# Eighty-two products of zeros between the warm-up and the first real product of a fused attention and gated feed-forward kernel

## The chip, the core and the metric

The kernel runs on one core of a Trainium2 chip. Its time is the device time of one execution in microseconds (us). The engines are TensorE (PE in the profile, its weight loads PEld), VectorE (DVE), ScalarE (ACT), GpSimd (POOL) and SyncE (SP, here a queue for DMAs alone); each runs its own instructions in order, and they wait for each other by semaphores.

## The reference

`x` has 2048 tokens of 448 numbers. Attention with 16 heads of 28 and a gated feed-forward block of width 1792 both read the same `x`; a gate per token mixes the two. All data are float32.

```python
x = A_x
g = _sigmoid((x * gate_w).sum(-1, keepdims=True))
# attention: 16 heads of 28
qkv = x @ wqkv
scores = einsum("bhqd,bhkd->bhqk", q, k) * 28 ** -0.5
o = einsum("bhqk,bhkd->bhqd", softmax(scores), v)
a = o @ wo
# feed-forward, 448 -> 1792 -> 448
gate = x @ W_gate
gate = gate * (gate > 0)
b = (gate * (x @ W_up)) @ W_down
return g * a + (1 - g) * b
```

## The kernel before

**Two forms of product.** A float32 product can go to TensorE in two ways here. In the split form a number is written as a high and a low part, each in a rounded 32-bit type (`F32R` in the code), and a product is the sum of three such products: high by high, low by high, high by low. Contractions over 448 rows take 11 instructions (`TERMS`, with the last half chunk packed). In the exact form the operands are plain float32 (`F32`, or `f32(...)`, which reads a rounded tile as float32), and one call of `matmul` does the whole product. The kernel uses the exact form only for probabilities by values (line 692, tile `po`): there the stationary operand is 32 columns wide, and four heads' blocks, j = 0 to 3, go to four strips of 32 partitions of one PSUM bank. `pv` runs for 32 visits (16 heads, two halves of the keys each) in two parts of 4 chunks by 4 blocks: 32 x 2 x 16 = 1024 calls of `matmul`.

**Stages.** (1) A warm-up: 11 bf16 products of a zeroed tile `warm` (line 496), which nobody reads. (2) Projections: `qk(tb, c)` makes 128 rows of queries and keys for a block of 512 tokens in 11 split products (line 454), `vproj` the values (line 469). What they read, `W` and `X`, is loaded by DMA and split into high and low parts by ScalarE (`act_high`, line 136) and VectorE (`low`, line 142); `split_first` does this chunk by chunk for the first block. (3) 32 rounds, one per head and half of the keys, whose order on TensorE is written out by hand in the strings `R0` to `R31`: score products (line 330), products for the row maxima (line 224), products of the feed-forward layer (line 633), and the exact ones (line 692). (4) The rest of the feed-forward layer (`down_mm`, line 927) and the output projection (line 886).

**What sets the order at the start.** Nothing is reordered: each engine gets its instructions in the order of the calls. Behind the warm-up come, on POOL, the identity matrix, four memsets of `K[0]`, `QS[0]`, `K[1]`, `QS[1]` (lines 503 and 504), eight memsets of `V` (lines 506 and 507), and behind those the DMAs that send the first projections to DRAM (lines 464 and 363). `QS[1]` holds the queries of head 1 later on. On ScalarE and VectorE come `split_first`, `split_w(*w1)`, then the two copies of the first projection out of PSUM (high part and low part, to `K[2]`, which serves as a staging buffer), and behind these the splits of the next blocks of `x`. The banks of PSUM: a pool `mx` of two tiles of two banks (used from the first row maxima on), `x` and `s` of two banks each. `ps_x("warm_ps")` takes a bank of `x`.

Of the kernel before, what the change touches and what calls it, by code (L numbers as in the profile page):

```python
# [8 lines left out]
F32 = mybir.dt.float32  # L9
# [9 lines left out]
P = 128  # L19
# [9 lines left out]
TB = 512  # L29
# [70 lines left out]
def gated_mix_kernel(ctx, tc, x, wq, wo, wgu, wd, out):  # L100
    nc = tc.nc
# [3 lines left out]
    psum = ctx.enter_context(tc.tile_pool(name="psum", bufs=1, space=PSUM))  # L105
# [3 lines left out]
    def f32(ap):  # L109
        return ap.bitcast(F32)  # L110
# [53 lines left out]
    QS = [vp.tile([P, 4, TB], F32R, name=f"Q{r}") for r in range(2)]  # L164
# [200 lines left out]
    with tc.tile_pool(name="qkv", bufs=1) as pa:  # L365
# [128 lines left out]
        ps = ps_x("warm_ps")  # L494
        for n in range(WARM):
            nc.tensor.matmul(ps, warm[:, :P], warm, start=True, stop=True)

        ident = const.tile([P, P], F32, name="ident")
        make_identity(nc, ident)
# [37 lines left out]
        for n, (f, *a) in enumerate(mixed):  # L537
# [29 lines left out]
            among, was = [], m  # L567
# [207 lines left out]
    for v, order in enumerate(ROUNDS):  # L775
# [4 lines left out]
        for o in order:  # L780
# [12 lines left out]
            elif o == "x":  # L793
                i, half, n = passes.pop(0)
# [228 lines left out]
```

## Time and profile before

| | |
|---|---|
| median of 2 runs | 1184.8 us (1184.59 to 1185.01) |
| profiled execution, device time | 1184.21 us |
| its span, first to last instruction | 1182.4 us |
| TensorE busy | 1175.0 us, 99% of the span |
| VectorE, ScalarE, GpSimd busy | 894.1, 877.2, 743.3 us |
| granted TensorE clock, mean | 0.999 |
| mean HBM traffic | 159 GB/s over the span |

How to read it: a line of a timeline gives the start and the length in us, the engine, the line of the kernel, the operation, output and input tiles, shapes, how many instructions were merged (x...), and in brackets how long the engine had been idle before and what ended that. Instructions of TensorE are pipelined: a product's own length (some 400 ns for a split one) is longer than the distance from its start to the next one's start, so costs are taken from such distances, or from a run of many products divided by their count.

### The profile page before, as it was taken

What the parts mean: (1) busy time and instruction counts of PE and PEld (TensorE: products, weight loads), DVE (VectorE), ACT (ScalarE), POOL (GpSimd) and SP (SyncE); (2) the same over time, 40 slices, a digit from 0 to 9 for tenths busy, and PEclk for the clock granted to TensorE, in tenths of its full rate; (3) what the DMA queues carried; (4) which work ended last, traced back from release to release, by engine and by line L of the source; (5) the groups of instructions that cost most, each with busy time, mean ns of one, the idle gap of its engine ahead of it and who ended that gap; (6) DMA issues with size and microseconds to landing.
All of it is one profiled execution on the core that took longest, in us unless ns stands there. A gap on an engine that the chain in (4) does not pass through costs nothing.

```text
span 1182.4 us, 17006 instructions
## 1 busy us (share of the span) xinstructions
PE 1175.0 (99%) x6183; PEld 821.2 (69%) x6183; DVE 894.1 (76%) x1173; ACT 877.2 (74%) x1054; POOL 743.3 (63%) x325
## 2 busy tenths in 40 slices
PE   9999999999999999999999999999999999999998
PEld 6886666666666666666666666666666667899997
DVE  6577898888988898989898888889898553444242
ACT  5237889899999988888888887888888885322121
POOL 5323667888988886777777766767676784422020
PEclk9999999999999999999999999999999999999999
DMA  9994565636373754343446535153444437644342
GB/s 322 280 394 142 186 210 172 185 124 196 117 216 108 205 167 139 119 128 92 119 136 212 140 102 153 49 152 109 139 154 156 129 100 231 209 152 118 115 134 75
DMA packets 70667, 188.85 MB, mean 160 GB/s; under 512 B 13958, under 2 KB 20558, under 8 KB 65678
## 3 DMA queue, kind: packets, MB, share of 16 engines
q1 hardware_dynamic: 65624, 167.31, 45.9%
q0 software_dynamic: 4480, 19.99, 4.5%
q8 instruction: 48, 0.79, 0.3%
q10 hardware_dynamic: 480, 0.47, 0.1%
q14 instruction: 35, 0.29, 0.1%
HBM read 126.96 MB, written 60.96 MB: 159 GB/s over the span
## 4 chain that ended last, share of the span: by engine, by line
PE 96%; DVE 1%; DMA 1%; ACT 1%; issue 0%; SPq 0%; DVEq 0%; ACTq 0%
PE gu L633 24%; PE s L330 20%; PE po L692 19%; PE acc L927 12%; PE sm L224 10%; PE v L469 3%; PE wo L886 3%; PE qk L641 3%; PE qk L454 2%; DVE r L280 1%; DMA wr<-wq 0%; DMA X<-x_d 0%; ACT P L336 0%; ACT V L336 0%; SPq L414 0%
## 5 line engine op out<-in xcount | busy, mean ns | idle before, releaser
L309 POOL TENSOR_TENSOR P<-P,rm 128x2048 f32<-128x2048 f32 x102 | 470.8, 4635 | 107.9 <-DVE rm L303 84.1
L633 PE MATMUL gu<-X,wg 128*128 128x512 f32 x1232 | 358.9, 395 | 0.1
L228 DVE TENSOR_REDUCE mx<-sm 128x1 f32<-128x1024 f32 x256 | 302.9, 1217 | 43.0 <-PE sm L224 42.1
L330 PE MATMUL s<-Q,K 128*128 128x512 f32 x1024 | 315.9, 403 | 1.7 <-DVE mx L228 0.9
L633 PEld LDWEIGHTS gu<-X,wg 128*128 128x128 f32 x1232 | 231.2, 188 | 57.6 <-issue 1.7
L330 PEld LDWEIGHTS s<-Q,K 128*128 128x128 f32 x1024 | 180.7, 188 | 82.4 <-DVE r L280 10.4
L336 ACT ACTIVATE P<-s 128x1024 f32<-128x1024 f32 x204 | 202.2, 1028 | 42.0 <-PE s L330 39.6
L692 PE MATMUL po<-P,V 128*32 128x512 f32 x1640 | 227.4, 594 | 0.0
L334 ACT ACTIVATE P<-s 128x1024 f32<-128x1024 f32 x206 | 201.4, 1040 | 14.1 <-PE s L330 13.1
L320 ACT ACTIVATE P<-P 128x1024 f32<-128x1024 f32 (+1 forms) x182 | 208.5, 1171 | 0.5 <-POOL P L309 0.2
L224 PE MATMUL sm<-K,Q 128*128 128x512 f32 x520 | 163.2, 400 | 0.1
L280 DVE SCALAR_TENSOR_TENSOR r<-s,r 128x1024 f32<-128x1024 f32 x124 | 151.6, 1223 | 13.6 <-ACT P L336 6.0
L692 PEld LDWEIGHTS po<-P,V 128*32 128x32 f32 x1640 | 62.6, 110 | 113.3 <-issue 109.6
L692 PE MATMUL po<-V 128*32 128x512 f32 x408 | 136.2, 594 | 0.0
L309 POOL TENSOR_TENSOR V<-V,rm 128x2048 f32<-128x2048 f32 x24 | 111.2, 4635 | 26.1 <-DVE rm L303 22.6
L224 PEld LDWEIGHTS sm<-K,Q 128*128 128x128 f32 x520 | 91.9, 188 | 34.1 <-ACT P L334 4.6
L136 ACT ACTIVATE hh<-hr 128x512 fp32r<-128x512 f32 x52 | 32.8, 632 | 109.5 <-PE acc L927 109.4
L142 DVE TENSOR_TENSOR hh<-hr,hh 128x512 fp32r<-128x512 f32 x52 | 47.3, 915 | 72.6 <-ACT hh L136 72.5
L927 PE MATMUL acc<-WD,hh 128*128 128x448 f32 x480 | 99.5, 366 | 0.0
L927 PEld LDWEIGHTS acc<-WD,hh 128*128 128x128 f32 x480 | 90.2, 188 | 7.3 <-DVE hh L142 0.2
L280 DVE SCALAR_TENSOR_TENSOR r<-s,P 128x1024 f32<-128x1024 f32 x50 | 61.1, 1223 | 33.3 <-ACT P L336 33.0
L295 DVE TRANSPOSE_TENSOR_REDUCE mn<-r 128x32 f32<-128x1024 f32 x63 | 78.1, 1239 | 1.3
(93 smaller groups left out, 1135.5 us busy)
## 6 DMA issues: line engine op xcount, KB each, us to landing
wg<-ws_d SPq DMA_DIRECT2D x42, 896.0 KB
K<-qk_d SPq DMA_DIRECT2D x32, 448.0 KB
X<-x_d SPq DMA_DIRECT2D x56, 256.0 KB
h_d<-h SPq DMA_DIRECT2D x56, 256.0 KB
Q<-qk_d SPq DMA_DIRECT2D x62, 224.0 KB
hr<-h_d SPq DMA_DIRECT2D x52, 256.0 KB
ws_d<-wg SPq DMA_DIRECT2D x14, 896.0 KB
x_d<-X POOLq DMA_DIRECT2D x8, 1024.0 KB, 15.2
```

Of the source, the lines that this page charges most:

```text
L224: nc.tensor.matmul(ps[:, c, :], Q[h][:, u * P:(u + 1) * P], K[h % 3][:, k0:k0 + TB], start=True, stop=True)
L228: nc.vector.tensor_reduce(to, ps, axis=AX.XY, op=OP.max)
L280: nc.vector.scalar_tensor_tensor(r, ps, -1.0, before, op0=OP.mult, op1=OP.min)
L295: nc.vector.tensor_reduce(MN[:, 1:3], R2.pop((v, j)).rearrange("p a (b r) -> p a b r", r=32), axis=AX.X, op=OP.min, apply_transpose=True)
L309: nc.gpsimd.tensor_tensor(QUAD[q], QUAD[q], m, op=OP.subtract)
L320: nc.scalar.activation(q, q, AF.Exp, scale=-SCALE)
L330: nc.tensor.matmul(ps[:, c], K[h % 3][:, k * P:(k + 1) * P], Q[h][:, j * TB:(j + 1) * TB], start=True, stop=True)
L334: nc.scalar.activation(dst, ps, AF.Exp, scale=SCALE)
L336: nc.scalar.activation(dst, ps, AF.Copy, scale=-1.0)
L633: nc.tensor.matmul(ps, WS[i][:, s, a], xf(i // NF, b), start=(n == 0), stop=(n == NT - 1))
L692: nc.tensor.matmul(po[32 * j:32 * j + 32], V[:, h // 4 % 2, k, h % 4], AT.pop((v, k, j)), start=(k == k0), stop=(k == k0 + NK // 2 - 1))
L927: nc.tensor.matmul(ACC[i // NF][t][:, :D], HH[i][:, a, t * P:(t + 1) * P], wd_high_low(f, b), start=(f == 0 and n == 0), stop=(f == NF - 1 ...
```

## The change

Behind the 11 warm-up products TensorE gets 82 calls of `matmul` more, in nine lots, ahead of the first real product. All read `z`, a quarter of `QS[1]` (128 x 512), which VectorE sets to zero first; they write the two tiles of the pool `mx`, and nobody reads what they write. In order: 8 split ones with 128 stationary columns; 8 exact ones of 128 columns; 4 split; 8 times four exact ones of 32 columns, in four strips of columns; 4 split; 8 times two exact ones of 64 columns, in two strips; 4 split; 4 exact ones of 32 columns, all in the first strip; 2 split. Each has 512 moving columns. That is 22 split and 60 exact ones (8 + 32 + 16 + 4).

```diff
         ps = ps_x("warm_ps")
         for n in range(WARM):
             nc.tensor.matmul(ps, warm[:, :P], warm, start=True, stop=True)
+
+        z = QS[1][:, 0]
+        nc.vector.memset(f32(z), 0.0)
+        four = [psum.tile([P, 2, TB], F32, tag="mx", bufs=2, name=f"four_{k}") for k in range(2)]
+        four = [t[:, k] for t in four for k in range(2)]
+
+        def tiles(z, columns, count, among=1):
+            for n in range(count):
+                for k in range(among):
+                    c = slice(k * columns, (k + 1) * columns)
+                    nc.tensor.matmul(four[n % 4][c], z[:, c], z, start=True, stop=True)
+
+        for t, columns, count, among in ((z, P, 8, 1), (f32(z), P, 8, 1), (z, P, 4, 1), (f32(z), 32, 8, 4), (z, P, 4, 1),
+                                         (f32(z), 64, 8, 2), (z, P, 4, 1), (f32(z), 32, 4, 1), (z, P, 2, 1)):
+            tiles(t, columns, count, among)
 
         ident = const.tile([P, P], F32, name="ident")
         make_identity(nc, ident)
```

On TensorE, at the program's start, the last warm-up product is followed before by the first projection (`qk_0`, which reads `X` and `W`):

```order
L496 LDWEIGHTS warm
L496 MATMUL warm_ps<-warm 128x512
L454 MATMUL qk_0_199<-X_119,W 128x512 x2
L454 MATMUL qk_0_199<-X_120,W 128x512
L454 MATMUL qk_0_199<-X_119,W 128x512 x2
```

and now by the products of zeros (`Q_108` is `QS[1]`; rows of split and exact ones of 128 columns read alike, and the first number of a shape is the count of stationary columns). From the middle of the fourth lot on, without the last two split ones, they are:

```order
L507 MATMUL four_157<-Q_108 32x512 x8
L507 MATMUL four_158<-Q_108 32x512 x8
L507 MATMUL four_157<-Q_108 128x512 x2
L507 MATMUL four_158<-Q_108 128x512 x2
L507 MATMUL four_157<-Q_108 64x512 x4
L507 MATMUL four_158<-Q_108 64x512 x4
L507 MATMUL four_157<-Q_108 64x512 x4
L507 MATMUL four_158<-Q_108 64x512 x4
L507 MATMUL four_157<-Q_108 128x512 x2
L507 MATMUL four_158<-Q_108 128x512 x2
L507 MATMUL four_157<-Q_108 32x512 x2
L507 MATMUL four_158<-Q_108 32x512 x2
```

What moved: all of TensorE's real work stands behind these rows, in its old order.

On POOL, at the same place, with the semaphores that a row waits for in brackets, before:

```order
L503 MEMSET K_105 32x2048
L504 MEMSET Q_108 32x2048
L506 MEMSET V 128x64x4 [waits Pool_49]
L507 MEMSET V 128x64 [waits Pool_49]
L506 MEMSET V 128x64x4
```

and now:

```order
L518 MEMSET K_105 32x2048
L519 MEMSET Q_108 32x2048 [waits DVE_49,PE_49]
L521 MEMSET V 128x64x4 [waits Pool_49]
L522 MEMSET V 128x64 [waits Pool_49]
L521 MEMSET V 128x64x4
```

The order on POOL is the old one, but the memset of `QS[1]` now waits for TensorE, because it overwrites a part of `z`; the memsets of `V` and the first DMAs to DRAM stand behind it in the same queue.

## The prediction

> **What bounds the kernel now.** I read the page first: busy shares, slices, and the chain that ended last.
>
> ```profile
> span 1182.4 us, 17006 instructions
> PE 1175.0 (99%) x6183; PEld 821.2 (69%) x6183; DVE 894.1 (76%) x1173; ACT 877.2 (74%) x1054; POOL 743.3 (63%) x325
> ...
> PEclk9999999999999999999999999999999999999999
> ...
> PE 96%; DVE 1%; DMA 1%; ACT 1%; issue 0%; SPq 0%; DVEq 0%; ACTq 0%
> ```
>
> TensorE is busy for 99% of the span and 96% of the chain: the kernel is as long as TensorE's queue. Whatever is put into that queue lengthens the kernel by its own time, unless TensorE would have waited then. So two things have to be found: what the 82 products take, and which waits of TensorE they cover. For the waits, first the timeline of the start, then the waits of TensorE from 10.4 us to the end:
>
> ```profile
> 0.87 0.27 DVE L493 MEMSET warm<- 128x256 uint32 x1 [0.87 <-PEq L1016]
> 1.20 4.88 PE L496 MATMUL warm_ps<-warm 128*128 128x512 bf16 x11 [1.20 <-DVE warm L493]
> 5.51 3.72 PE L454 MATMUL qk<-X,W 128*128 128x512 f32 x10
> 9.39 0.83 PE L454 MATMUL qk<-X,W 128*128 128x512 f32 x2 [0.16 <-DVE X L142]
> 10.41 27.98 PE L454 MATMUL qk<-X,W 128*128 128x512 f32 x120 [0.20 <-DVE W L142]
> ...
> PE s L330 <- DVE mx L228: 0.9, 1, 0.9
> PE s L330 <- DVE mn L590: 0.4, 1, 0.4
> PE s L330 <- ACT P L334: 0.2, 1, 0.2
> ```
>
> The first 12 real products are strung out from 5.51 to 10.41 us, because ScalarE and VectorE still split their operands. The 13th starts at 10.41; from there 120 run without a hole, and TensorE waits for only some 1.5 us in all the rest. The 13th product is therefore the mark: what it starts later, everything behind it starts later.
>
> **What one added product costs.** *Split, 128 columns.* The same form fills the row at 10.41: 27.98 / 120 = 0.233 us from one to the next. Early on it is slower. The same tile's rows in two windows of 1.2 us (the columns are PE, PEld, DVE and ACT busy time with counts, then clock and DMA):
>
> ```profile
> 5.50:6.70 1.20, 1.19 (x2) 0.95 (x3) 0.00 (x0) 0.00 (x0) 1.00 1.03 366
> 6.70:7.90 1.20, 1.20 (x7) 0.89 (x5) 0.00 (x0) 0.00 (x0) 1.00 1.03 347
> ```
>
> Two products, then seven: the profile has no clock sample ahead of that, but the warm-up's 11 in 4.88 us are about 0.43 us apart, and up to about 6.7 us everything goes at roughly half speed. The warm-up's tile is zeros too, so zeros wake the clock.
>
> *Exact.* No row shows an exact product of 128 or 64 columns in this kernel; the nearest are those of 32 columns in four strips (line 692):
>
> ```profile
> L692 PE MATMUL po<-P,V 128*32 128x512 f32 x1640 | 227.4, 594 | 0.0
> L692 PE MATMUL po<-V 128*32 128x512 f32 x408 | 136.2, 594 | 0.0
> ...
> 143.10 7.00 PE po L692 x64
> ...
> 113.63 0.40 PE L641 MATMUL qk<-X,wb 128*128 128x512 f32 x1
> 113.96 3.64 PE L692 MATMUL po<-P,V 128*32 128x512 f32 x32
> 117.42 0.61 PE L692 MATMUL po<-V 128*32 128x512 f32 x3
> 117.44 0.59 PE L692 MATMUL po<-P,V 128*32 128x512 f32 x1
> 117.85 0.60 PE L692 MATMUL po<-V 128*32 128x512 f32 x3
> 117.87 0.59 PE L692 MATMUL po<-P,V 128*32 128x512 f32 x1
> ...
> 120.44 0.59 PE L692 MATMUL po<-V 128*32 128x512 f32 x1
> 120.44 0.59 PE L692 MATMUL po<-P,V 128*32 128x512 f32 x1
> 120.97 0.27 PE L236 MATMUL mt<-ident,m 128*8 128x128 f32 x1
> ```
>
> 1640 + 408 = 2048 rows, but the code calls line 692 only 1024 times: an exact product is two records. And the records come in steps of four, one per strip: 117.42, 117.85, one step each 0.43 us (64 records, 16 steps, in 7.00 us). So the four strips run side by side, and a strip's product takes two steps, 0.86 us. Changing the form costs a little: the step at 113.96 starts 0.33 us behind a split product, not 0.233; and 120.97 is 0.53 behind the last step, not 0.43. That is 0.10 us for each change.
>
> For four strips of 32 columns this is a row of the very form that is added. Four strips together are the whole width of 128, so I take two steps of 0.43 us for one of 128 columns as well. The bound below is two records at the split form's spacing, 0.47; the bound above adds a weight load in front of each record, 0.188 us by the rows that follow, 1.24. For two strips of 64 I take two steps for the pair, between 0.47 and, one behind the other, 1.72. The four single ones of 32 columns share a strip, so each must follow the one before: 0.86 each. The Trainium skill ("FP8 and Floating Point Precision", TensorE Precision Notes) says that true FP32 takes four passes through the array, whatever the width; four half-steps of 0.215 us make the same 0.86, though no row of before shows it at 64 or 128 columns.
>
> Weight loads: are they hidden?
>
> ```profile
> L330 PEld LDWEIGHTS s<-Q,K 128*128 128x128 f32 x1024 | 180.7, 188 | 82.4 <-DVE r L280 10.4
> L692 PEld LDWEIGHTS po<-P,V 128*32 128x32 f32 x1640 | 62.6, 110 | 113.3 <-issue 109.6
> ...
> 114.42 0.13 PEld L692 LDWEIGHTS po<-P,V 128*32 128x32 f32 x4 [0.30 <-issue]
> 114.84 0.13 PEld L692 LDWEIGHTS po<-P,V 128*32 128x32 f32 x4 [0.30 <-issue]
> ```
>
> Four loads lie at the head of each step, under the products that have just begun (a step is 0.43 us either way), and a load of 0.188 us plus a product would not fit into the split form's 0.233. So yes. The Trainium skill ("TensorE: Matmul & The Clock Gate", Part 3, The mechanism) speaks against that: a weight load overlaps a running product only where their row groups differ, and all of these use all 128 rows. By that rule every load would show, and the real split products could not be 0.233 us apart; the trace disagrees, and I let the rule stand only for the exact ones of 64 and 128 columns, which no row shows (a rival below).
>
> **The sum.** The last warm-up product starts at about 1.20 + 10 x 0.427 = 5.47, so the first added one can start at about 5.9 (VectorE zeroes `z` right after `warm`, whose memset took 0.27 us; it is there long before). From 5.9:
>
> - 22 split: two before 6.7 at 0.43, 20 at 0.233: 0.86 + 4.66 = 5.5 us.
> - 8 exact of 128: 16 steps. 8 fours of 32: 16 steps. 8 pairs of 64: 16 steps. 4 single ones: 8 steps. 56 x 0.43 = 24.1 us.
> - 8 changes of form at 0.10: 0.8 us.
>
> Together 30.4 us; the first real product starts at about 36.3. All its operands have been split for 25 us by then (the wait at 10.41 was the last), so 12 products take 12 x 0.233 = 2.8 us and the 13th starts at 39.1 instead of 10.41: 28.7 us later. The cover is 1.7 us (from 5.9 to 10.41 there were 4.5 us for 2.8 us of work); nothing else of the 30.4 us is hidden.
>
> **What else moves.** The memset of `QS[1]` on POOL waits for the last product of zeros, and behind it queue the memsets of `V` and the first DMAs to DRAM:
>
> ```profile
> 6.60 1.81 POOL L504 MEMSET Q<- 32x2048 f32 x1
> 8.47 0.32 POOL L506 MEMSET V<- 128x256 f32 x1
> ...
> 10.31 0.21 POOL L507 MEMSET V<- 128x64 f32 x1
> 12.15 0.82 POOL L464 DMA_DIRECT2D qk_d<-K  x1 [1.62 <-DVE K L142]
> ...
> 10.20 0.58 ACT L136 ACTIVATE K<-qk 128x512 fp32r<-128x512 f32 x1
> 11.14 0.69 DVE L142 TENSOR_TENSOR K<-qk,K 128x512 fp32r<-128x512 f32 x1
> ```
>
> From 6.60 to 10.52 that is 3.9 us, so POOL is free 4 us after the first real product's start. What its DMA then waits for comes after 11 x 0.233 = 2.6 us of products, 0.1 until ScalarE sees them, and 1.6 from 10.20 to VectorE's end at 11.83: 4.3 us. The DMA is not late, and if it were by a few tenths, nobody reads its data before the row maxima, which stand behind all projections of queries and keys. ScalarE and VectorE stand still behind the first projection's copies, which now come 28 us later, so the splits of the next blocks gain no lead; distances from there on are the old ones. Of the 1.5 us of later waits, which end on VectorE's and ScalarE's answers to TensorE, I count nothing as saved; at best 1.5.
>
> **Total.** Span 1182.4 + 28.7 = 1211.1; the profiled execution lies 1184.21 - 1182.4 = 1.8 us above its span: 1212.9. The median of the runs is 0.6 above that execution's time, so a run should read about 1213, +2.4%. A difference of 2%, 23.7 us (1208.5), is about what a measurement of this kernel can surely tell from no change. My own case runs from 1210 (later waits saved, no cost for a change of form, half a microsecond of clock) to 1216 (the clock wakes up to 3 us later, at half a microsecond each; 0.02 us more for each wide record).
>
> **Rivals.**
>
> - *Not slower by 2%: wide exact records stream like split ones.* The 0.43 us step may belong to four separate strips that share something, not to the record. If a record of 128 or 64 columns takes 0.233, the 16 + 16 steps lose 32 x 0.197 = 6.3 us: 1206.6. It decides once the wide steps save 4.5 us together. For it: no row shows such a record. Against: the record `mt` (a transpose, 8 columns, 128 moving) lasts 0.27 us and a `po` one, with 512 moving, 0.59: 0.32 us for 384 columns more is the same 0.43 per 512, without any other strip beside it. Chance 0.09.
> - *Two strips of 64 don't run side by side.* Then 16 steps more, 6.9 us: 1219.9. Against: four strips do. Chance 0.08.
> - *Weight loads of wide exact records show.* 16 x 0.188 for 128 columns, 16 x about 0.149 (between the two rows) for 64: 5.4 us, 1218.4. Chance 0.05.
> - *The clock falls during the four single products*, which occupy a quarter of the columns for 3.4 us. As at the start it would take some 5.5 us (1.20 to 6.7) to come back, at half speed: 2.7 us, and up to 1.7 for the singles themselves: up to 1217. No row of before has TensorE so thinly used for so long. Chance 0.05.
> - *The products are dropped, as nobody reads them.* The order has all rows; 0.01, at 1185.
>
> **Numbers.** My case has 0.72, at 1213. The range must leave out no more than 0.2: from 1206, which takes in the cheap wide records, to 1219, which takes in the visible loads and the clock and ends short of the pairs in series. Faster by 2%: 0.01 for what I haven't thought of. Same: the first rival, the last, and its neighbourhood: 0.11. Slower: 0.88.
>
> **What would show it.** In the profile after: 142 more TensorE records (22 + 2 x 60), starts 0.43 us apart in the exact lots of 128 and 64, four strips' records at one time in the fourth lot, the first real product at about 36 us, no wait ahead of the 13th, POOL's first DMA within half a microsecond of VectorE's copy, and the same distances as before from there to the end. A start of the first real product before 32 us, or a wait of TensorE of over 1 us between 40 and 75 us, would make the prediction wrong.

## The result, and the profile after

The changed kernel takes 1215.9 us (1215.88 to 1215.93, two runs) against 1184.8 (1184.59 to 1185.01): a ratio of 1.026, 95% interval 1.024 to 1.028. The forecast was 1213, between 1206 and 1219.

The page of the changed kernel, the rows that answer to those of before:

```profile
span 1214.1 us, 17294 instructions
PE 1204.1 (99%) x6325; PEld 831.9 (69%) x6325; DVE 895.7 (74%) x1174; ACT 877.4 (72%) x1054; POOL 743.8 (61%) x325
...
PE 92%; DMA 3%; DVE 2%; ACT 1%; issue 1%; SPq 0%; POOL 0%; ACTq 0%; DVEq 0%; POOLq 0%
```

TensorE has 142 records more (6325 - 6183), as many weight loads, and 29.1 us more of busy time. But its share of the chain that ended last fell from 96% to 92%, and DMAs rose to 3%. A share of the chain is not a length of waiting, but it hints that not all of the 31.7 us that the span grew by are products. The timeline of TensorE at the start, and POOL's rows behind its new wait:

```profile
1.20 4.02 PE L496 MATMUL warm_ps<-warm 128*128 128x512 bf16 x11 [1.20 <-DVE warm L493]
4.87 30.46 PE L507 MATMUL four<-Q 128*128 128x512 f32 x142
35.16 11.03 PE L454 MATMUL qk<-X,W 128*128 128x512 f32 x47
...
35.38 1.81 POOL L519 MEMSET Q<- 32x2048 f32 x1 [28.71 <-PE four L507]
...
39.55 0.83 POOL L464 DMA_DIRECT2D qk_d<-K  x1 [0.23 <-issue]
```

The zeros fill 4.87 to 35.16 us, 30.3 us. The same by lots, as busy time of TensorE in nine windows (the count includes a record that reaches in from the window before):

```profile
4.86:6.89 2.03, 2.02 (x8) 1.00 1.07 359
6.89:13.99 7.10, 7.10 (x18) 1.00 0.74 262
13.99:14.77 0.78, 0.78 (x4) 1.00 0.00 0
14.77:21.78 7.01, 7.01 (x66) 1.00 0.01 2
21.78:22.90 1.12, 1.12 (x8) 1.00 0.00 0
22.90:29.92 7.02, 7.02 (x33) 1.00 0.00 0
29.92:31.04 1.12, 1.12 (x6) 1.00 0.00 0
31.04:34.59 3.55, 3.55 (x9) 1.00 0.00 0
34.59:35.16 0.57, 0.57 (x3) 1.00 0.00 0
```

In order: 8 split; 8 exact of 128 columns (16 records, and the first split one behind them); the rest of 4 split; 8 fours of 32; 4 split; 8 pairs of 64; 4 split; 4 single ones; 2 split. The exact lots of 128, of four strips and of two strips cost the same, 7.0 us each, 0.43 us a step. The split lots between strips take 1.12 us, though four split products take 0.92 elsewhere (0.231 each).

The waits of TensorE, the view that shows what the sum did not have:

```profile
PE acc L942 <- DVE hh L142: 1.6, 1, 1.6
PE warm_ps L496 <- DVE warm L493: 1.2, 1, 1.2
PE s L330 <- DVE mx L228: 0.9, 1, 0.9
PE gu L648 <- DMA X<-x_d: 0.8, 1, 0.8
PE sm L224 <- DMA Q<-qk_d: 0.7, 1, 0.7
```

Three of these (`acc`, `gu`, `sm`) are new (the prediction shows the waits of before); the one on `warm` and the one on `mx` are before's. If each real product's start is set against that of before, the 13th comes 27.5 us later, and the distance then jumps at three places: by 0.65 at 74 us, where the first row maxima wait for a load of queries (46 us by the clock of the profile before); by 0.95 at 449 us (420), where the feed-forward products wait for the next block of `x`; and by 2.1 at 1161 to 1164 us (1131), where the down projection waits for hidden values; 0.4 is won back between. From there to the end it grows by 0.9 more without any wait. The last run of products on the chain, before and after, in the chain of work in order of time (start, us, what, how many):

```profile
1144.52 34.06 PE acc L927 x168
```

```profile
1175.56 34.73 PE acc L942 x168
```

The same 168 products take 0.67 us longer, 0.207 instead of 0.203 us each. It ends at 31.7.

### The profile page after: what moved, and what is told of

It reads as the page before. It is cut to its first block, busy times and chain, and to the rows that moved or that the text cites. A ratio compares the mean times of both kernels' runs of the same rounds, so it can differ in the third digit from the quotient of the medians.

```text
span 1214.1 us, 17294 instructions
## 1 busy us (share of the span) xinstructions
PE 1204.1 (99%) x6325; PEld 831.9 (69%) x6325; DVE 895.7 (74%) x1174; ACT 877.4 (72%) x1054; POOL 743.8 (61%) x325
## 4 chain that ended last, share of the span: by engine, by line
PE 92%; DMA 3%; DVE 2%; ACT 1%; issue 1%; SPq 0%; POOL 0%; ACTq 0%; DVEq 0%; POOLq 0%
PE gu L648 23%; PE s L330 19%; PE po L707 19%; PE sm L224 10%; PE acc L942 10%; PE wo L901 3%; PE qk L656 3%; PE four L507 2%; PE v L469 2%; DVE r L280 1%; DMA Q<-qk_d 1%; DMA hr<-h_d 1%; ACT P L336 0%; DMA ox<-x 0%; DMA X<-x_d 0%
## 5 line engine op out<-in xcount | busy, mean ns | idle before, releaser
L228 DVE TENSOR_REDUCE mx<-sm 128x1 f32<-128x1024 f32 x256 | 302.6, 1216 | 44.3 <-PE sm L224 43.5
```

The costliest lines, as they stand in the source:

```text
L228: nc.vector.tensor_reduce(to, ps, axis=AX.XY, op=OP.max)
```

## Experiments: where the last 4 us come from

That the products cost 30.3 us can be read off the trace. Open was why three waits far behind them are new. Theory A, called D in the later runs: the delay shifts later DMAs in a fixed way. B: POOL's new wait. C: chance. The runs of one set share their runs of the kernel before.

**The changed kernel once more, and the kernel before once more.** No edit.

> The changed kernel once more. TensorE's first 13 real products come 27.5 us later than before in the first profile, the span is 31.7 us longer; the other 4.2 us are three waits that before has not (at about 74, 449 and 1161 us). Theory A (the delay shifts later DMAs in a fixed way): the same three waits within 0.2 us each, 1216. Theory B (the memset of QS[1] on POOL, which waits for the zeros, makes the first DMAs late): the same, 1216. Theory C (chance: DMAs land earlier or later from one execution to the next): other waits at other places, the time between 1212 and 1218.

> The kernel before once more. A and B: 1184.8, no wait of TensorE over 0.3 us at 46, 420 and 1131 us. C: some wait of half a microsecond or more at a place where the first profile has none. In all cases the clock, which woke at 6.7 us before and 4.2 us after, may wake at another time; 1 us of it is 0.5 us of the time.

Measured: 1215.7 us, ratio 1.026 (1.025 to 1.028), and 1185.3, ratio 1.000 (0.999 to 1.001). The repeated changed kernel waits at the same three places, for 1.0, 1.7 and 1.0 us; the repeated one of before has nothing there. The places are fixed, the sizes are not: C falls as an account of the places, and A's "within 0.2 us" fails.

**Zeros from another tile.**

```diff
-        z = QS[1][:, 0]
+        z = K[2][:, :TB]
```

> The zeros lie in K[2], which is next written behind the first projection in any case, so that POOL's memsets wait for nothing; TensorE's products are the same. A: 1216, the three waits stay. B: the waits go, 1212. C: 1212 to 1218, waits at other places than in the repeated run.

Measured: 1215.0 us (1213.8 to 1217.2), ratio 1.026 (1.024 to 1.028). POOL's memset no longer waits, and the waits at the loads of queries (0.9 us) and of `x` (1.3) are there; the third was absent in this execution. B falls: POOL's new wait costs nothing that can be measured, as forecast.

**The same delay in split form alone.**

```diff
-        for t, columns, count, among in ((z, P, 8, 1), (f32(z), P, 8, 1), (z, P, 4, 1), (f32(z), 32, 8, 4), (z, P, 4, 1),
-                                         (f32(z), 64, 8, 2), (z, P, 4, 1), (f32(z), 32, 4, 1), (z, P, 2, 1)):
+        for t, columns, count, among in ((z, P, 131, 1),):
```

(and `z` in `K[2]` as above).

> 131 split products of zeros (from K[2]) in place of the 82 calls: 131 x 0.2315 = 30.3 us, the same delay in one form. A: 1216 with the same three waits. B: 1212. C: 1212 to 1218. If the exact form leaves something behind that costs later, it is under 1213 and r2 is not.

Measured: 1213.2 us (1212.5 to 1213.3), ratio 1.024 (1.022 to 1.025): 2.5 us less than the changed kernel, with only 0.4 us less of zeros (29.9 us). The third wait was gone, the one for `x` 0.6. Neither form nor delay was an obvious reason, so I looked at what else differed, and found the instructions themselves.

**A new theory, F: the fetches of instructions.** The DMA queues of the page, before and after:

```profile
q8 instruction: 48, 0.79, 0.3%
...
q8 instruction: 50, 0.82, 0.3%
```

0.79 MB in 48 packets is 16 KB a packet; TensorE's records of before, 6183 products and as many loads, make 12366 instructions, 258 for each packet. So a packet brings TensorE some 256 instructions, and comes after every 128 products or so. The pages of the runs below bear this out: the queue has 48 packets with nothing added, 49 with 28 or 256 instructions more, and 50 with 262 to 290. The changed kernel has 2 x 142 = 284 more, one packet and 28 instructions (called the remainder below), so all later packets come some 14 products earlier in the work. In the changed kernel one of them falls on the moment at which a load of 1 MB of values (`V<-v_d`) ends, which by the clock of the profile before is 414 us instead of 417. What hangs on that is in the waits of SyncE's queue around it, before, after, and in the repeated run of the changed kernel:

```profile
SPq L628 <- DMA V<-v_d: 1.1, 1, 1.1
```

```profile
SPq L643 <- DMA V<-v_d: 2.1, 1, 2.1
```

```profile
SPq L643 <- DMA V<-v_d: 2.9, 1, 2.9
```

The loads of the next block of `x` stand in that queue behind a wait for the load of values; when that lands later, they are issued later, and TensorE, which has no slack there, waits. The third place is alike: a load of attention output (`or<-o_d`) on which ScalarE waits, with the split of the hidden values behind it. ScalarE's rows, before and after:

```profile
1126.33 1.06 ACT L136 ACTIVATE on<-or 128x1024 fp32r<-128x1024 f32 x1 [2.29 <-DMA or<-o_d]
1127.29 0.62 ACT L136 ACTIVATE hh<-hr 128x512 fp32r<-128x512 f32 x1
```

```profile
1157.21 1.06 ACT L136 ACTIVATE on<-or 128x1024 fp32r<-128x1024 f32 x1 [4.48 <-DMA or<-o_d]
1158.18 1.14 ACT L136 ACTIVATE hh<-hr 128x512 fp32r<-128x512 f32 x2
```

Here a packet comes at the issue of the load, which takes longer. SyncE's row for it, before and after:

```profile
1120.30 0.43 SPq L870 DMA_DIRECT2D or<-o_d  x1
```

```profile
1148.99 1.52 SPq L885 DMA_DIRECT2D or<-o_d  x1
```

Before, the issue takes 0.43 us. In the changed kernel it takes 1.52 and ends at 1150.51, 0.36 us behind the end of an instruction packet (1148.72 to 1150.15 in the trace's DMA records).

Five runs were made to tell F from D.

**Few zeros, the same remainder.** `(z, P, 14, 1)` in place of `(z, P, 131, 1)`.

> Only 14 split products of zeros (from K[2]): 28 more instructions (a weight load and a product each), the same remainder as the changed kernel's 284 = 256 + 28; TensorE's instructions are fetched in pieces of 16 KB, 256 instructions. The zeros end at about 8.3 us and the 13th real product starts at about 11.1, 0.7 us later than before. Theory F (the fetches fall at other places of the work, in front of loads that TensorE needs): waits at the loads of X (about 421 us) and at the split of the last hidden values (about 1132 us) as in the changed kernel, 1 to 3 us together; 1187 to 1188.5. Theory D (the waits come from the 30 us of delay): no such waits, 1185.7 to 1186.5.

Measured: 1188.7 us (1186.4 to 1190.4), ratio 1.0029 (1.0019 to 1.0038). 3.4 us of zeros, and the waits for `x` (1.6 us), hidden values (1.4) and queries (0.8). The median lies 0.2 us above F's range, and 2.2 above D's.

**The changed kernel with whole packets.**

```diff
-        for t, columns, count, among in ((z, P, 8, 1), (f32(z), P, 8, 1), (z, P, 4, 1), (f32(z), 32, 8, 4), (z, P, 4, 1),
-                                         (f32(z), 64, 8, 2), (z, P, 4, 1), (f32(z), 32, 4, 1), (z, P, 2, 1)):
+        for t, columns, count, among in ((z, P, 2, 1), (f32(z), P, 8, 1), (z, P, 2, 1), (f32(z), 32, 8, 4), (z, P, 2, 1),
+                                         (f32(z), 64, 8, 2), (z, P, 1, 1), (f32(z), 32, 4, 1), (z, P, 1, 1)):
```

> The changed kernel with 14 of its 22 split products of zeros left out (2, 2, 2, 1, 1 remain): 256 more instructions, a whole fetch, so that the fetches fall where they fell before. 14 x 0.2315 = 3.2 us fewer: 1212.4 by the delay alone (theory D, with the same waits at the loads of X and at 1158 us). F: these two waits shrink by 1 to 3 us, 1209.5 to 1211.5; the wait of the first row maxima (0.7 to 1.1 us) stays in both.

Measured: 1210.8 us (1209.7 to 1211.9), ratio 1.0215 (1.0199 to 1.0231); 4.9 us less than the changed kernel's 1215.7, where the 14 products are 3.2. The third wait is gone, the one for `x` is down to 0.5, the one for queries stays at 1.0.

**145 split products**, remainder 34, in place of 131.

> 145 split products of zeros instead of 131: 290 more instructions, remainder 34, nearly the changed kernel's; 131 had remainder 6. 14 x 0.2315 = 3.2 us more: 1216.4 by the delay alone (D). F: the wait at about 1162 us comes as in the changed kernel (1 to 2 us), and the one at the loads of X grows: 1217.5 to 1219.

Measured: 1217.6 us (1216.1 to 1220.4), ratio 1.0272 (1.0247 to 1.0297): 4.5 us above the 131, of which 3.2 are the products. The waits for `x` and for hidden values (1.2 and 0.6 us) are there; the second is smaller than F said.

**No zeros at all: the warm-up cut finer.** The kernel before with

```diff
-        for n in range(WARM):
-            nc.tensor.matmul(ps, warm[:, :P], warm, start=True, stop=True)
+        for n in range(25):
+            nc.tensor.matmul(ps[:, :225], warm[:, :P], warm[:, :225], start=True, stop=True)
```

> The kernel before, without products of zeros behind the warm-up; only the warm-up itself is cut finer: 25 products of 225 columns in place of 11 of 512 (5625 moving columns instead of 5632, so the same time at the warm-up's rate). 14 more products and 14 more weight loads: 28 more instructions and no delay. Theory F (place of the instruction fetches): waits at the loads of X (about 421 us) and at about 1131 us, 1 to 3 us together, none at the first row maxima; 1186.3 to 1188. Theory D (delay): 1185.2, no such waits.

Measured: 1187.0 us (1185.5 to 1188.6), ratio 1.0016 (1.0006 to 1.0025): 1.6 us slower with the warm-up as long as before; the first real product starts at 5.76 instead of 5.51 and the 13th at 10.03, earlier than before. TensorE's waits:

```profile
PE gu L633 <- DMA X<-x_d: 1.2, 1, 1.2
...
PE sm L224 <- DMA Q<-qk_d: 0.6, 1, 0.6
PE acc L927 <- DVE hh L142: 0.5, 1, 0.5
```

The waits for `x` and hidden values need no delay. The one for queries came too, which F had not said.

**The changed kernel in exact form alone.**

```diff
-        for t, columns, count, among in ((z, P, 8, 1), (f32(z), P, 8, 1), (z, P, 4, 1), (f32(z), 32, 8, 4), (z, P, 4, 1),
-                                         (f32(z), 64, 8, 2), (z, P, 4, 1), (f32(z), 32, 4, 1), (z, P, 2, 1)):
+        for t, columns, count, among in ((f32(z), P, 14, 1), (f32(z), 32, 8, 4), (f32(z), 64, 8, 2), (f32(z), 32, 4, 1)):
```

> The changed kernel with its 22 split products of zeros replaced by 6 more exact ones of 128 columns (22 x 0.2315 = 5.1 us against 6 x 0.858 = 5.1 us): the same delay within 0.5 us, 264 more instructions instead of 284, remainder 8 instead of 28. F: as with 131 split products (remainder 6) the wait at about 1160 us shrinks under 0.6 us and the time is 1212.5 to 1214. D: 1215 to 1216, with the changed kernel's waits.

Measured: 1213.6 us (1212.6 to 1216.0), ratio 1.0244 (1.0230 to 1.0258), F's range in the median. Its profiled execution was the longest of the four, 1216.0, with a wait of 0.6 us for hidden values, at F's edge, and the clock awake only at 6.9 us.

**What the times alone say.** The runs with 14 products and with the finer warm-up (ten and eleven executions) rule D out: D's figures, at most 1186.5 and 1185.2, lie below their 95% intervals. In the other three, of four executions each, D's figure (1212.4 and 1216.4; 1215 to 1216) lies inside the interval; there the waits in the traces tell the theories apart, not the times.

**All kernels together.** From the trace's DMA records: us from the issue of the load of values to the end of the instruction packet nearest to it, to the start of the load's last packet in that burst, and to the issue of the second load of `x`; then TensorE's waits for `x` and for hidden values, and how long SyncE's issue of the load `or` took.

```
kernel                   more instr.  packet  last start  x issued  wait x  wait hidden  or issue
before                        0         9.99     6.30       7.02      0       0            0.43
before, again                 0        14.12     5.88       6.63      0       0            0.43
whole packets               256        14.06     5.88       6.65      0.5     0            0.43
131 split                   262         6.84     5.88       6.64      0.6     0            0.43
exact only                  264         7.34     6.08       6.85      0.5     0.6          0.43
changed                     284         6.75     6.74       8.03      0.8     1.6          1.52
changed, again              284         7.47     7.45       8.76      1.7     1.0          0.97
zeros from K[2]             284         7.19     7.17       8.46      1.3     0            0.57
145 split                   290         6.84     6.82       8.12      1.2     0.6          0.81
14 split                     28         7.95     7.94       9.24      1.6     1.4          1.31
warm-up in 25 pieces         28         7.38     7.36       8.62      1.2     0.5          1.09
```

In the last six the load's last packet starts within 0.02 us of the end of the instruction packet: it stood behind it. In the first five it did not, and the loads of `x` are issued 1 to 2.6 us earlier. All kernels with remainder 28 or 34 are in the second group, all with 0 to 8 in the first, and among each are short and long delays (0, 27 and 30 us in the first, 0, 3, 30 and 33 in the second). With 262 and 264 more instructions a packet came at nearly that time too, but not in front of the values' last one; in those kernels TensorE's waits lie between.

The last column divides the kernels in the same way. In the last six the issue of `or` takes 0.57 to 1.52 us and ends 0.36 or 0.37 us behind the end of an instruction packet, in every one of them; in the first five it takes 0.43, and no packet ends in the 3 us before it.

**What stays open.** The wait for the first queries (0.6 to 1.1 us) is in all kernels but the two runs of before, also with whole packets and with no delay. From the 11th real product to the first row maximum it is 36.4 and 36.7 us in the two runs of before and 36.7 to 37.1 in all others. So part of the wait is the cover of the start handed back (the products between now come without holes, the loads of queries do not come sooner), and up to 0.7 us is loads that are there later, for which no run here gave the reason. The wait for `x` has a part that no packet explains: with whole packets the loads of `x` are issued as early as in the repeated run of before, and yet there is a wait of 0.5 us. The wait for hidden values is explained in part. The late issue is at most 1.1 us; from the issue's end to its landing the load then takes 4.2 to 6.4 us, in both groups, and the runs give no reason for that. The run with zeros from `K[2]` (remainder 28) had the shortest and no wait; the one in exact form alone (remainder 8) had one of the two longest and a wait of 0.6 us. After that wait the last 220 products or so run at 0.207 us each in four of the six profiles that have it (the changed kernel twice, 145 split, exact only), at 0.203 in the other two and in all without it; what sets this was not tried. It is up to 0.9 us of an execution, and so part of what the medians differ by.

## Why the prediction was right, point by point

- *TensorE is the bound, what is put into its queue adds to the end.* Right.
- *An exact product is two records, two steps of 0.43 us, at every width; strips run side by side; single ones in a strip follow each other.* Right in all four lots: 16 wide records took 7.10 less the split one of 0.23, 6.87 us; the fours 7.01, the pairs 7.02, the singles 3.55. The rivals with cheap wide records (1206.6), pairs in series (1219.9) and visible weight loads (1218.4) fall: with a load in front of each record the wide lot would have been 3 us longer. So does the rule of the Trainium skill that went with the last ("TensorE: Matmul & The Clock Gate", Part 3, The mechanism): all these loads use all rows, and none shows. The page of the Trainium skill that the prediction cites for four passes ("FP8 and Floating Point Precision", TensorE Precision Notes) names no width; the 0.86 us at 128, 64 and 32 columns is four times 0.215, and that it is the same at each width is what these lots show.
- *0.10 us for each change of form.* Near in sum, wrong in place. The wide exact lot has no such cost at either end. The cost comes with the change from 128 columns to strips and back: the three strip lots (7.01, 7.02 and 3.55) are 0.12 to 0.15 us more than 16, 16 and 8 steps of 0.429, and the split lots beside them are 0.1 us longer at each such side (1.12 against 0.92 between two strip lots). Six changes cost 1.0 us together, 0.17 each, where the sum had eight at 0.10.
- *30.4 us of zeros.* 30.3, with errors that cancel: nothing ran at half rate, as the clock woke before the zeros came (11 warm-up products in 4.02 instead of 4.88 us), which saved 0.4 us; the first zeros took 0.2 more, and the changes of form 0.2 more.
- *The 13th real product 28.7 us later, at 39.1.* It started at 37.94, 27.5 later. The step that was off is the start of the zeros, 4.87 instead of 5.9. Of that 0.6 us is the clock (the last warm-up product starts at 4.84, before at 5.44). The other 0.4 is a misreading: the sum put a whole step behind the last warm-up product, but the next one's record starts 0.03 us behind it, as the first real product's did before (0.07); half of this comes back as the 0.2 of the first zeros. In nine further profiles TensorE came to full rate between 4.1 and 6.9 us.
- *The clock does not fall during the single products.* Right: 3.55 us for 8 steps, and the split ones behind at 0.23.
- *POOL's first DMA is not late.* Right: it starts 0.32 us behind the end of VectorE's copy, as before, with POOL idle for 0.23 us on nothing but issue, and the run without POOL's wait is no faster.
- *"Distances from there on are the old ones", and nothing of the later waits changes.* Wrong, and the one term that was missing. The distance grew by 4.2 us in the profiled execution, from waits of 0.65, 0.95 and 2.1 us, less 0.4, and 0.9 from the slower last products. The first is part of the 1.7 us of cover, which the sum booked as a gain to the end though the next load on the way did not come sooner (36.65 and 36.66 us from the 11th product to the first row maximum in these two profiles). What the 28 instructions too many cost is 1.3 to 1.7 us by three comparisons of medians (4.9 - 3.2 = 1.7 with whole packets; 4.5 - 3.2 = 1.3 from 131 to 145; 1.6 without zeros), of which only the last stands clear of the noise by itself. The remainder of the 4.2 us is open, as said above.
- *The signs of being wrong.* The first real product came at 35.16, not before 32. The wait between 40 and 75 us was 0.70 us in the first profile, under the 1 us that was set; in the repeated run it was 1.03, just over. "No wait ahead of the 13th" held.

By its own terms the sum is 1212.9 + 0.6 = 1213.5 rather than 1213. The total came out at +2.6% for +2.4%. The cost of the zeros was right by its mechanism; that the total is this near is partly luck, as the early start of the zeros and the missing waits are of opposite sign, and the range held it because it had been widened for other things.

## What to carry to other kernels

Where one engine is the whole chain, a sum over its queue in steps read from neighbouring rows is good to a per cent, also for a form that the trace does not show, if one counts records and not calls. What such a sum lacks is at the loads without slack: look in the waits of the DMA queue for an issue that waits for another load's landing, since there a microsecond from anywhere goes straight to the end. And added instructions have a second price beside their own time: they move every later instruction fetch, so before one explains a change of a tenth of a per cent by its logic, one should try the same number of instructions without the change.

## What the runs showed of the hardware

- Fourteen more products and weight loads in the warm-up, with the first real product at 5.76 us instead of 5.51, cost 1.6 us of 1185 (ratio 1.0016, 1.0006 to 1.0025). Packets of 16 KB of TensorE's instructions (0.9 to 1.9 us each in the eleven profiles) come at other moments: a data load's last packet stood behind one (wait for `x` 1.2 us), and SyncE's issue of another load took 1.09 us instead of 0.43 and ended just behind one (wait for hidden values 0.5 us). The 0.6 us wait for queries is not explained. The Trainium skill ("Runtime: NRT & Kernel Launch", Instruction fetch mechanics) has blocks of 16 KiB or 256 instructions, as the trace does, and calls the cost of crossing one mostly hidden; for the fetching engine that holds here (in the profile of before, the three waits of TensorE that the prediction shows behind the 13th real product, some 1.5 us, all end on other engines), for the data loads beside it it does not.
- An exact product of 128 columns takes 0.86 us, as much as four of 32 in four strips or two of 64 in two, and as one of 32 alone: width costs nothing, strips left empty do.
- After a wait the same product stream can settle at 0.207 us a product instead of 0.203, for 35 us to the end.
- A change between split and exact products of 128 columns costs nothing; one between 128 columns and strips costs 0.17 us each way (1.0 us for six).
